# Linear attention and a routed feed-forward block on one core: y's product placed between kv and M, and the first k weights on another queue

## The chip, the core and the metric

The kernel runs on one core of a Trainium2 chip. A core has a matrix engine (TensorE, in the profile PE, its weight loads PEld), a vector engine (VectorE, DVE), a scalar engine (ScalarE, ACT), GpSimd (POOL) and SyncE (SP), which here only issues DMAs. Each engine takes its instructions in order, and they wait for each other by semaphores. Products land in PSUM, a small memory of banks, and have to be evicted from there by VectorE or ScalarE. The metric is the device time of one execution in microseconds, lower is better.

## What is computed

The input x has 2048 tokens of 640 values, in bf16. Three things are added up: x, a linear attention of the normalized x, and a routed block which again gives x, plus an update for eight tokens.

```python
xn = _layernorm(x)
# A: 32 heads of 20
q, k, v = split(xn @ wqkv)
phi = lambda t: jnp.where(t > 0, t + 1, jnp.exp(t)) + 1e-6
kv  = einsum("bhsd,bhse->bhde", phi(k), v)
z   = einsum("bhsd->bhd", phi(k))
a   = (einsum(phi(q), kv) / (einsum(phi(q), z) + 1e-6)) @ wo
# B: the 8 tokens with the largest r = xn @ w_r
sel = xn[argsort(-r)[:8]]
y   = ((silu(sel @ w_gate) * (sel @ w_up)) @ w_down) * sigmoid(r_sel)
b   = xn + scatter(y to the 8 tokens)
out = x + a + b
```

## The kernel before

The tokens are worked in 16 tiles of 128 (`T`, index t), the 640 columns in 5 chunks (`KC`).

**The start.** Loads go out on two queues: SP's (`nc.sync.dma_start`) and ScalarE's (`nc.scalar.dma_start`), L104 to L113. The k weights `wk` come in two pieces: chunks 2 to 4 on ScalarE's queue (L108), chunks 0 and 1 on SP's (L109). Each tile is normalized: VectorE takes statistics of the two halves (`ln_half`, L163) and joins them (`ln_aggr`, L167); the root and, from tile 2 on, the reciprocal are made on GpSimd (L171 to L179), for tiles 0 and 1 (`LN_FAST`) partly on VectorE (L171 for tile 0, L175, L189); `ln_norm` (L191) writes xn. TensorE needs the transposed xnT: tiles 0 to 2 are transposed on TensorE (`tr_tile`, L200) and evicted (`tr_evict`, L206), later tiles by a transposing DMA on SP (L196). One column of wk holds w_r, put there through a small product (L287, L288).

**The loop** over t has k = xn wk (L236), the Gram products ga of phi(k) and xn (L259), and q (L248); ScalarE makes exp and relu (L213, L216) and VectorE joins them (L225). SP also issues the later loads in a fixed order, between the transposes (`late_loads`, L343), and writes xn + x to a copy in DRAM, xcp (L363). The Gram matrix GT = xn^T phi(k) takes the place of v: kv is then wv^T GT.

**The last third** runs in the order in which it is written. Selection of the eight tokens on VectorE and GpSimd; gbA and gbC (L489, L590), the rest of the Gram matrix; gate and up of the eight tokens (gu, L606); hm, transposed on TensorE as ph after tile 8 of gbC (L642) and multiplied into hT (L643). GT's last columns are evicted from gbC on ScalarE (L650). Then y = hT wd (py, 48 products, L655), copied on VectorE (L663), and added by an indirect DMA from GpSimd to eight rows of xcp (L664). SP then reloads x from xcp in six pieces (L669). TensorE goes on with kv in eight blocks of 80 columns (L678), evicted in three groups by VectorE into a masked, spread form kvT (L688), and M = kv wo in five chunks (L728), evicted on ScalarE and, for chunks 2 and 4, on VectorE (L743). `norm(j)` (L632) divides a quarter of phi(q) by its denominator, in place, on VectorE; four of them come before the output sums. An output block t (L749) is 5 x 2 products of pqT and M in PSUM, rotating over four places (A, B, the banks D0 and D1, C); VectorE adds x (L757) and a store goes out on SP or ScalarE's queue in turn (L768). The last block is worked in three pieces (L770 to L776).

Of the kernel before, what the change touches and what calls it, by code (L numbers as in the profile page):

```python
# [8 lines left out]
P = 128  # L9
S = 2048  # L10
D = 640
# [3 lines left out]
T = S // P  # L15
KC = D // P
FC = F // P
# [27 lines left out]
def kernel(  # L45
# [62 lines left out]
    nc.scalar.dma_start(wk[:, 2:KC, 0:D], wqkv_v[:, 2:KC, D : 2 * D])  # L108
    nc.sync.dma_start(wk[:, 0:2, 0:D], wqkv_v[:, 0:2, D : 2 * D])  # L109
# [55 lines left out]
    def ln_aggr(t):  # L165
# [5 lines left out]
        (nc.vector if t == 0 else nc.gpsimd).tensor_scalar(  # L171
            out=sq[:, 0:1], in0=mv[:, 1:2], scalar1=EPS_BF16, scalar2=None, op0=ALU.add
        )
        if t < LN_FAST:
            nc.vector.tensor_copy(sc[:, 0:1], mv[:, 0:1])  # L175
# [28 lines left out]
    def tr_evict(t, ptr, lo, hi, copy):  # L204
        src = ptr[:, 0:D].rearrange("p (k f) -> p k f", k=KC)
        copy(xnT[:, lo:hi, t * P : (t + 1) * P], src[:, lo:hi, :])  # L206
# [81 lines left out]
    nc.scalar.copy(wk[:, :, D], prep[:, 0:KC])  # L288
    ln_half(1, 1)
    ln_aggr(1)  # L290
    ln_half(2, 0)
    ln_half(2, 1)
    ln_norm(1)
# [86 lines left out]
    tr_evict(1, tr1a, 0, 2, nc.vector.tensor_copy)  # L380
    tr_tile(1, tr1b, 2, KC)
    tr_evict(1, tr1b, 2, KC, nc.scalar.copy)
# [255 lines left out]
    for t in range(2, 9):  # L638
        gb2(t)
# [8 lines left out]
    for t in range(9, T):  # L648
        gb2(t)
    nc.scalar.copy(GT[:, :, TBLK:D], gbC[:, 0:D].rearrange("p (c f) -> p c f", c=KC))  # L650
    py = bank("D0", "py")
    for fc in range(FC):
        j, b = fc // 3, fc % 3
        for i in range(4):
            nc.tensor.matmul(  # L655
                py[32 * i : 32 * i + 32, 0:QW],
                lhsT=hT[:, 4 * b + j, :],
                rhs=wd[:, fc, i * QW : (i + 1) * QW],
                start=(fc == 0), stop=(fc == FC - 1),
                tile_position=(0, 32 * i),  # L660
            )
    y_sb = sb([P, QW], BF16, "y_sb")
    nc.vector.tensor_copy(y_sb[:], py[:, 0:QW])  # L663
    nc.gpsimd.indirect_dma_start(  # L664
        out=xcp[:], out_offset=bass.IndirectOffsetOnAxis(ap=rowu[:, 0:1], axis=0),
        in_=y_sb[:], in_offset=None, compute_op=ALU.add,
    )
    for a, b in ((0, 1), (1, 2), (2, 4), (4, 8), (8, 12), (12, 16)):
        nc.sync.dma_start(x_sb[:, a:b, :], xcp_v[:, a:b, :])  # L669


    pkv = (bank("D1", "pkv0"), bank("D0", "pkv1"), pair("B", "pkv2"))
    groups = (range(0, NEB, 2), (1, 3), (5, 7))
# [12 lines left out]
    def kv_evict(i):  # L686
        n, lo, w = len(groups[i]), groups[i][0], KC * 2 * PAD
        nc.vector.tensor_tensor(  # L688
            out=kvT[:, PAD : PAD + NEB * w].rearrange("e (b m c) -> e b m c", b=NEB, m=KC)[
                :, lo : groups[i][-1] + 1 : 2, :, 0:PAD  # L690
# [9 lines left out]
    norm(0)  # L700

# [18 lines left out]
    pm = {}  # L720

    def m_pass(m, i):
        if i == 0:
            pm[m] = Acc("CABDC"[m], f"M{m}")
        for a, b in halves:
            for g in range(4):
                o = PAD + ((2 * g + i) * KC + m) * 2 * PAD - i * PAD
                nc.tensor.matmul(  # L728
                    pm[m].at(a, b)[32 * g : 32 * g + 32, :],
                    lhsT=kvT[:, o : o + 2 * PAD],  # L730
                    rhs=wo[:, 2 * g + i, a:b],
                    start=(i == 0), stop=(i == 1),
                    tile_position=(0, 32 * g),
                )

    m_pass(0, 0)
    m_pass(1, 0)
    for m in range(KC):
        if m > 1:
            m_pass(m, 0)  # L740
        m_pass(m, 1)
        for a, b in pm[m].spans:
            (nc.vector.tensor_copy if m in (2, 4) else nc.scalar.copy)(M[:, m, a:b], pm[m].at(a, b))  # L743
    for j in range(1, NTB):
        norm(j)
# [13 lines left out]
    for t in range(T):  # L759
        o_t = work.tile([P, D], BF16, tag=("ek", "rk", "eq", "rq")[t % 4], name=f"o_t{t}")  # L760
        if t < T - 1:
            po = Acc("ABDC"[t % 4], f"o{t}")
# [5 lines left out]
            (nc.sync, nc.scalar)[t % 2].dma_start(out_v[:, t, :], o_t[:])  # L768
        else:
# [41 lines left out]
```

## Time and profile before

| | us |
|---|---|
| median of three runs | 113.37 (113.35 to 115.64) |
| the profiled execution | 113.7 |
| its span in the profile | 112.0 |
| TensorE busy | 105.6 (94%) |
| VectorE busy | 85.8 (77%) |
| ScalarE busy | 54.9 (49%) |
| GpSimd busy | 40.2 (36%) |

The span runs from the first to the last recorded instruction or transfer; 1.7 us of the execution lie outside it. A row of the timeline gives the start in us from the span's beginning, the length in us, the engine, the line, the operation, its output and input tiles, the shapes and how many are merged in the row; in brackets stands how long the engine sat idle before it, and what ended that. A row of a transfer with "KB" gives its size and the time from issue to landing. PSUM and SBUF tiles are named as in the code. An engine with "q" behind its name (SPq, ACTq) is its instruction queue, where DMAs are issued.

### The profile page before, as it was taken

The numbers are of one execution on the slowest core, as the hardware profiler recorded it, in microseconds if no ns is written. First come the engines' busy times: TensorE is split into PE (matmuls) and PEld (weight loads), VectorE is DVE, ScalarE is ACT, GpSimd is POOL, SyncE is SP. The second block draws the span as 40 slices with busy tenths as digits, with TensorE's granted clock in tenths as the row PEclk, the third lists the DMA queues.
The fourth block names the chain that finished last, engine by engine and source line by source line (L and its number), as shares of the span: only waits on it lengthen the run. The fifth ranks groups of instructions, "written<-read, shape, count | busy, mean of one in ns | idle before, by whom it ended". The sixth has DMA issues, their size and how long they took to land.

```text
span 112.0 us, 3000 instructions
## 1 busy us (share of the span) xinstructions
PE 105.6 (94%) x1183; PEld 69.5 (62%) x1183; DVE 85.8 (77%) x199; ACT 54.9 (49%) x101; POOL 40.2 (36%) x90
## 2 busy tenths in 40 slices
PE   6889999999799999999999999999999999999990
PEld 2345866777377766777766644358886555555560
DVE  6898799887998889867999887933139999756581
ACT  4038987777577787777977745086016000000000
POOL 5328495998799757590000000430051000000000
PEclk9999999999999999999999999999999999999999
DMA  3998179997989999996999730039322799943333
GB/s 77 328 376 272 30 112 343 216 273 154 148 191 322 252 115 298 277 305 181 292 372 385 279 117 4 0 117 310 112 81 21 214 341 378 336 147 117 117 117 117
DMA packets 25359, 23.09 MB, mean 206 GB/s; under 512 B 10625, under 2 KB 24065, under 8 KB 25345
## 3 DMA queue, kind: packets, MB, share of 16 engines
q1 hardware_dynamic: 22784, 20.53, 67.9%
q10 hardware_dynamic: 2384, 2.33, 6.0%
q0 software_dynamic: 176, 0.04, 0.6%
q8 instruction: 9, 0.15, 0.6%
q14 instruction: 6, 0.04, 0.1%
HBM read 14.94 MB, written 5.81 MB: 185 GB/s over the span
## 4 chain that ended last, share of the span: by engine, by line
PE 65%; DMA 10%; issue 9%; DVE 7%; ACT 2%; SPq 2%; POOL 1%; POOLq 0%; DVEq 0%
PE q L248 20%; PE k L236 19%; PE o L749 10%; PE gaC L259 6%; DMA wk<-in_A_wqkv_dram 4%; PE gaD L259 3%; DMA xcp<-y_sb,rowu 3%; DMA x_sb<-xcp 3%; PE gbA L489 2%; DVE o_t L757 2%; DVE pqT L632 1%; SPq L669 1%; PE zp L462 1%; PE o14a L749 1%; PE o10a L749 1%
## 5 line engine op out<-in xcount | busy, mean ns | idle before, releaser
L248 PEld LDWEIGHTS <-wq 128*128 128x128 bf16 x400 | 24.3, 117 | 3.5 <-issue 0.2
L236 PE MATMUL k<-wk,xnT 128*128 128x512 bf16 (+1 forms) x160 | 24.7, 300 | 1.5 <-ACT eq L213 0.8
L248 PE MATMUL q<-xnT,wq 128*128 128x128 bf16 x400 | 24.9, 219 | 0.0
L749 PEld LDWEIGHTS <-pqT 128*128 128x128 bf16 x165 | 12.8, 98 | 9.7 <-issue 0.4
L236 PEld LDWEIGHTS <-xnT 128*128 128x128 bf16 x160 | 12.5, 98 | 9.7 <-DMA xnT<-xn 0.9
L225 DVE SCALAR_TENSOR_TENSOR pk<-ek,rk 128x640 bf16<-128x640 bf16 x16 | 13.2, 824 | 4.4 <-ACT rk L216 4.2
L213 ACT ACTIVATE eq<-q 128x640 bf16<-128x640 f32 x16 | 11.2, 703 | 10.3 <-PE q L248 10.3
L749 PE MATMUL o<-M,pqT 128*128 128x512 bf16 x110 | 15.8, 299 | 0.3 <-DVE o_t L757 0.3
L163 DVE BATCH_NORM_STATS2 st<-x_sb 128x6 f32<-128x320 bf16 x32 | 14.1, 479 | 0.3 <-DMA x_sb<-in_A_x_dram 0.3
L225 DVE SCALAR_TENSOR_TENSOR pqT<-eq,rq 128x640 bf16<-128x640 bf16 x16 | 13.2, 823 | 0.2 <-ACT rq L216 0.2
L176 POOL TENSOR_TENSOR sq<-sq,half 128x1 bf16<-128x1 bf16 x16 | 12.4, 776 | 2.3 <-DVE sc L175 1.0
L213 ACT ACTIVATE ek<-k 128x640 bf16<-128x640 f32 x16 | 11.3, 705 | 2.2 <-PE k L236 1.1
L757 DVE TENSOR_TENSOR o_t<-o,x_sb 128x640 bf16<-128x640 f32 x11 | 8.8, 820 | 3.2 <-PE o L749 3.2
L178 POOL TENSOR_TENSOR sc<-sq,neg 128x1 f32<-128x1 bf16 x14 | 10.9, 776 | 1.1
L216 ACT ACTIVATE rq<-q 128x640 bf16<-128x640 f32 x16 | 11.2, 700 | 0.0
L216 ACT ACTIVATE rk<-k 128x640 bf16<-128x640 f32 x16 | 11.2, 699 | 0.0
L537 POOL COPY xsT<-xnT 128x5 bf16 x8 | 2.3, 353 | 21.2 <-DVE icol L551 21.2
L259 PE MATMUL gaC<-pk,xn 128*128 128x512 bf16 x32 | 9.5, 378 | 0.0
L191 DVE TENSOR_SCALAR xn<-x_sb,sc 128x640 bf16<-128x640 bf16 (+2 forms) x17 | 6.9, 409 | 2.2 <-POOL sc L179 2.1
L171 POOL TENSOR_SCALAR sq<-mv 128x1 bf16<-128x1 bf16 x15 | 4.7, 311 | 9.0 <-DVE mv L167 9.0
L489 PE MATMUL gbA<-pk,xn 128*128 128x512 bf16 x32 | 7.3, 380 | 0.0
L360 DVE TENSOR_TENSOR x_sb<-x_sb,xn 128x640 bf16<-128x640 bf16 x16 | 7.0, 482 | 0.0
(152 smaller groups left out, 118.6 us busy)
## 6 DMA issues: line engine op xcount, KB each, us to landing
xcp<-x_sb SPq DMA_DIRECT2D x4, 640.0 KB, 4.1
x_sb<-in_A_x_dram SPq DMA_DIRECT2D x3, 640.0 KB, 6.0
wd<-in_B_w_down_dram SPq DMA_DIRECT2D x2, 960.0 KB, 6.6
x_sb<-xcp SPq DMA_DIRECT2D x3, 640.0 KB, 6.8
wg<-in_B_w_gate_dram SPq DMA_DIRECT2D x2, 768.0 KB, 6.0
wu<-in_B_w_up_dram SPq DMA_DIRECT2D x2, 768.0 KB, 5.5
out_dram<-o_t SPq DMA_DIRECT2D x8, 160.0 KB, 2.3
out_dram<-o_t ACTq DMA_DIRECT2D x7, 160.0 KB, 1.9
```

Source lines behind the costliest of these rows:

```text
L163: nc.vector.bn_stats(out=stat[t][:, h, :], in_=x_sb[:, t, h * HW : (h + 1) * HW])
L176: nc.gpsimd.tensor_tensor(out=sq[:, 1:2], in0=sq[:, 0:1], in1=half[:], op=ALU.pow)
L178: nc.gpsimd.tensor_tensor(out=sc[:, 1:2], in0=sq[:, 1:2], in1=neg1[:], op=ALU.pow)
L213: nc.scalar.activation(e[:], ps[:, 0:D], AF.Exp)
L216: nc.scalar.activation(r[:], ps[:, 0:D], AF.Relu)
L225: nc.vector.scalar_tensor_tensor(out=dst, in0=ea, scalar=1.0, in1=ra, op0=ALU.min, op1=ALU.add)
L236: nc.tensor.matmul(ps[:, a:b], lhsT=xnT[:, kc, t * P : (t + 1) * P], rhs=wk[:, kc, a:b], start=(kc == 0), stop=(kc == KC - 1),)
L248: nc.tensor.matmul(ps[:, m * P : (m + 1) * P], lhsT=wq[:, kc, m::KC], rhs=xnT[:, kc, t * P : (t + 1) * P], start=(kc == 0 and m in (0, 4)) ...
L259: nc.tensor.matmul(gaC[:, c * TBLK : (c + 1) * TBLK] if c < 2 else gaD[:], lhsT=xn[:, t, c * P : (c + 1) * P], rhs=pk[:, t, 0:TBLK], start ...
L489: nc.tensor.matmul(gbA[:, (c - 3) * TBLK : (c - 2) * TBLK], lhsT=xn[:, t, c * P : (c + 1) * P], rhs=pk[:, t, 0:TBLK], start=(t == 0), stop ...
L749: nc.tensor.matmul(ps, lhsT=pqT[:, m, t * P : (t + 1) * P], rhs=M[:, m, a:b], start=(m == 0), stop=(m == KC - 1),)
L757: nc.vector.tensor_tensor(out=o_t[:, a:b], in0=ps, in1=x_sb[:, t, a:b], op=ALU.add)
```

## The change

Several edits are made together.

- At the start, chunks 0 to 2 of wk are loaded on ScalarE's queue and chunks 3 and 4 on SP's. The sum under tile 1's root is made on VectorE, as tile 0's; the casts of the means of tiles 0 and 1 are made on ScalarE. The copy of the w_r column comes behind the statistics of tile 1 in the text, which puts it behind tile 1's cast on ScalarE. Tile 1 is normalized between the two halves of tile 2's statistics. The two evictions of tile 1's transposition change engines.
- hm is transposed after tile 11 of gbC, not after tile 8.
- y's product, its copy, the scatter and the reloads of x move from ahead of kv to behind it; the copy is made on ScalarE, and y's place in PSUM is the pair A.
- kv's blocks are grouped 0, 2, 4, then 1, 3, 5, then 6, 7, where it was 0, 2, 4, 6, then 1, 3, then 5, 7.
- M is worked one chunk at a time, without the early first pass over chunks 0 and 1.
- Norms 1 and 2 stay ahead of the output sums; norm 3 comes behind the addition of output block 4.
- The places in PSUM rotate as B, A, D, C, and of the last block's three stores the second goes out on ScalarE's queue and the third on SP's.

```diff
@@ -105,8 +105,8 @@
     nc.scalar.dma_start(x_sb[:, 0, HW:D], x_v[:, 0, HW:D])
     for t in (1, 2):
         nc.sync.dma_start(x_sb[:, t, :], x_v[:, t, :])
-    nc.scalar.dma_start(wk[:, 2:KC, 0:D], wqkv_v[:, 2:KC, D : 2 * D])
-    nc.sync.dma_start(wk[:, 0:2, 0:D], wqkv_v[:, 0:2, D : 2 * D])
+    nc.scalar.dma_start(wk[:, 0:3, 0:D], wqkv_v[:, 0:3, D : 2 * D])
+    nc.sync.dma_start(wk[:, 3:KC, 0:D], wqkv_v[:, 3:KC, D : 2 * D])
     nc.scalar.dma_start(wq[:, 2:KC, :], wqkv_v[:, 2:KC, 0:D])
     nc.sync.dma_start(x_sb[:, 3, :], x_v[:, 3, :])
     nc.sync.dma_start(wq[:, 0:2, :], wqkv_v[:, 0:2, 0:D])
@@ -168,11 +168,11 @@
         sc = work.tile([P, 2], F32, tag="sc", name=f"sc{t}", bufs=4)
         sq = work.tile([P, 2], BF16, tag="sq", name=f"sq{t}", bufs=4)
         scal[t] = sc, sq
-        (nc.vector if t == 0 else nc.gpsimd).tensor_scalar(
+        (nc.vector if t < LN_FAST else nc.gpsimd).tensor_scalar(
             out=sq[:, 0:1], in0=mv[:, 1:2], scalar1=EPS_BF16, scalar2=None, op0=ALU.add
         )
         if t < LN_FAST:
-            nc.vector.tensor_copy(sc[:, 0:1], mv[:, 0:1])
+            nc.scalar.copy(sc[:, 0:1], mv[:, 0:1])
         nc.gpsimd.tensor_tensor(out=sq[:, 1:2], in0=sq[:, 0:1], in1=half[:], op=ALU.pow)
         if t >= LN_FAST:
             nc.gpsimd.tensor_tensor(out=sc[:, 1:2], in0=sq[:, 1:2], in1=neg1[:], op=ALU.pow)
@@ -285,12 +285,12 @@
     tr_evict(0, trb, 2, KC, nc.scalar.copy)
     prep = bank("D0", "prep").bitcast(BF16)
     nc.tensor.transpose(prep[:, 0:KC], wrow[:], ident[0:KC, 0:KC])
-    nc.scalar.copy(wk[:, :, D], prep[:, 0:KC])
     ln_half(1, 1)
     ln_aggr(1)
+    nc.scalar.copy(wk[:, :, D], prep[:, 0:KC])
     ln_half(2, 0)
+    ln_norm(1)
     ln_half(2, 1)
-    ln_norm(1)
     ln_aggr(2)
 
     iof = sb([P, 32], F32, "iof")
@@ -377,9 +377,9 @@
     kp = k_mm(0, "A")
     tr1a, tr1b = bank("D1", "tr1a").bitcast(BF16), pair("C", "tr1b").bitcast(BF16)
     tr_tile(1, tr1a, 0, 2)
-    tr_evict(1, tr1a, 0, 2, nc.vector.tensor_copy)
+    tr_evict(1, tr1a, 0, 2, nc.scalar.copy)
     tr_tile(1, tr1b, 2, KC)
-    tr_evict(1, tr1b, 2, KC, nc.scalar.copy)
+    tr_evict(1, tr1b, 2, KC, nc.vector.tensor_copy)
     ln_stats(3)
     ker = k_phi(0, kp)
     kp = k_mm(1, "B")
@@ -635,7 +635,7 @@
             op=ALU.mult,
         )
 
-    for t in range(2, 9):
+    for t in range(2, 12):
         gb2(t)
     ph = bank("D1", "ph").bitcast(BF16)
     for b in range(3):
@@ -645,32 +645,13 @@
         in0=ph[:, 0:FJ].rearrange("p (n c) -> p n c", c=32)[:, :, 0:C],
         in1=gtb[:].unsqueeze(1).to_broadcast([P, FC, C]), op=ALU.mult,
     )
-    for t in range(9, T):
+    for t in range(12, T):
         gb2(t)
     nc.scalar.copy(GT[:, :, TBLK:D], gbC[:, 0:D].rearrange("p (c f) -> p c f", c=KC))
-    py = bank("D0", "py")
...
-    for a, b in ((0, 1), (1, 2), (2, 4), (4, 8), (8, 12), (12, 16)):
-        nc.sync.dma_start(x_sb[:, a:b, :], xcp_v[:, a:b, :])
-
-
-    pkv = (bank("D1", "pkv0"), bank("D0", "pkv1"), pair("B", "pkv2"))
-    groups = (range(0, NEB, 2), (1, 3), (5, 7))
+
+
+    pkv = (bank("D0", "pkv0"), bank("D1", "pkv1"), pair("B", "pkv2"))
+    groups = ((0, 2, 4), (1, 3, 5), (6, 7))
 
     def kv_mm(i):
         for n, b in enumerate(groups[i]):
@@ -684,10 +665,11 @@
                 )
 
     def kv_evict(i):
-        n, lo, w = len(groups[i]), groups[i][0], KC * 2 * PAD
+        n, w = len(groups[i]), KC * 2 * PAD
+        lo, step = groups[i][0], groups[i][1] - groups[i][0]
         nc.vector.tensor_tensor(
             out=kvT[:, PAD : PAD + NEB * w].rearrange("e (b m c) -> e b m c", b=NEB, m=KC)[
-                :, lo : groups[i][-1] + 1 : 2, :, 0:PAD
+                :, lo : groups[i][-1] + 1 : step, :, 0:PAD
             ],
             in0=pkv[i][0:EB, 0 : n * EB].rearrange("e (b c m) -> e b m c", b=n, m=KC),
             in1=mask80[:].rearrange("e m h j -> e m (h j)").unsqueeze(1).to_broadcast([EB, n, KC, PAD]),
@@ -698,6 +680,26 @@
         kv_mm(i)
         kv_evict(i)
     norm(0)
+
+    py = pair("A", "py")
+    for fc in range(FC):
+        j, b = fc // 3, fc % 3
+        for i in range(4):
+            nc.tensor.matmul(
+                py[32 * i : 32 * i + 32, 0:QW],
+                lhsT=hT[:, 4 * b + j, :],
+                rhs=wd[:, fc, i * QW : (i + 1) * QW],
+                start=(fc == 0), stop=(fc == FC - 1),
+                tile_position=(0, 32 * i),
+            )
+    y_sb = sb([P, QW], BF16, "y_sb")
+    nc.scalar.copy(y_sb[:], py[:, 0:QW])
+    nc.gpsimd.indirect_dma_start(
+        out=xcp[:], out_offset=bass.IndirectOffsetOnAxis(ap=rowu[:, 0:1], axis=0),
+        in_=y_sb[:], in_offset=None, compute_op=ALU.add,
+    )
+    for a, b in ((0, 1), (1, 2), (2, 4), (4, 8), (8, 12), (12, 16)):
+        nc.sync.dma_start(x_sb[:, a:b, :], xcp_v[:, a:b, :])
 
     M = sb([P, KC, D], BF16, "M", tag="wq")
     halves = ((0, TBLK), (TBLK, D))
@@ -717,32 +719,24 @@
             i = a // TBLK
             return self.banks[i][:, a - i * TBLK : b - i * TBLK]
 
-    pm = {}
-
-    def m_pass(m, i):
-        if i == 0:
-            pm[m] = Acc("CABDC"[m], f"M{m}")
+    for m in range(KC):
+        pm = Acc("CBADC"[m], f"M{m}")
         for a, b in halves:
-            for g in range(4):
-                o = PAD + ((2 * g + i) * KC + m) * 2 * PAD - i * PAD
-                nc.tensor.matmul(
-                    pm[m].at(a, b)[32 * g : 32 * g + 32, :],
-                    lhsT=kvT[:, o : o + 2 * PAD],
-                    rhs=wo[:, 2 * g + i, a:b],
-                    start=(i == 0), stop=(i == 1),
-                    tile_position=(0, 32 * g),
-                )
-
-    m_pass(0, 0)
-    m_pass(1, 0)
-    for m in range(KC):
-        if m > 1:
-            m_pass(m, 0)
-        m_pass(m, 1)
-        for a, b in pm[m].spans:
-            (nc.vector.tensor_copy if m in (2, 4) else nc.scalar.copy)(M[:, m, a:b], pm[m].at(a, b))
-    for j in range(1, NTB):
-        norm(j)
+            for i in range(2):
+                for g in range(4):
+                    o = PAD + ((2 * g + i) * KC + m) * 2 * PAD - i * PAD
+                    nc.tensor.matmul(
+                        pm.at(a, b)[32 * g : 32 * g + 32, :],
+                        lhsT=kvT[:, o : o + 2 * PAD],
+                        rhs=wo[:, 2 * g + i, a:b],
+                        start=(i == 0), stop=(i == 1),
+                        tile_position=(0, 32 * g),
+                    )
+        copy = nc.vector.tensor_copy if m in (2, 4) else nc.scalar.copy
+        for a, b in pm.spans:
+            copy(M[:, m, a:b], pm.at(a, b))
+    norm(1)
+    norm(2)
 
 
     def out_mm(t, ps, m, a, b):
@@ -759,21 +753,23 @@
     for t in range(T):
         o_t = work.tile([P, D], BF16, tag=("ek", "rk", "eq", "rq")[t % 4], name=f"o_t{t}")
         if t < T - 1:
-            po = Acc("ABDC"[t % 4], f"o{t}")
+            po = Acc("BADC"[t % 4], f"o{t}")
             for m in range(KC):
                 for a, b in halves:
                     out_mm(t, po.at(a, b), m, a, b)
             for a, b in po.spans:
                 out_add(t, po.at(a, b), o_t, a, b)
             (nc.sync, nc.scalar)[t % 2].dma_start(out_v[:, t, :], o_t[:])
+            if t == 4:
+                norm(3)
         else:
             for i in range(3):
                 a, b = LAST[i : i + 2]
-                ps = pair("CAB"[i], f"o_last{i}")[:, 0 : b - a]
+                ps = pair("CBA"[i], f"o_last{i}")[:, 0 : b - a]
                 for m in range(KC):
                     out_mm(t, ps, m, a, b)
                 out_add(t, ps, o_t, a, b)
-                (nc.scalar, nc.sync, nc.scalar)[i].dma_start(out_v[:, t, a:b], o_t[:, a:b])
+                (nc.scalar, nc.scalar, nc.sync)[i].dma_start(out_v[:, t, a:b], o_t[:, a:b])
 
 
 def two(ap):
```

42 lines of the change are left out of this document (19 added, 23 removed).

## The prediction

> **What bounds the kernel now.** I read the page's busy times first, then TensorE's waits, then its weight loads in order of time.
>
> ```profile
> span 112.0 us, 3000 instructions
> ```
>
> ```profile
> PE 105.6 (94%) x1183; PEld 69.5 (62%) x1183; DVE 85.8 (77%) x199; ACT 54.9 (49%) x101; POOL 40.2 (36%) x90
> ```
>
> TensorE is at work in 94% of the span. The change takes no product away, so it can gain only what TensorE waits, and lose only what it makes TensorE wait. The longest wait of the products in the main loop (who waited for whom, total, times, longest), and the weight load of the same product (start, length, engine, line, operation, count, idle before it):
>
> ```profile
> PE k L236 <- ACT eq L213: 0.8, 1, 0.8
> ```
>
> ```profile
> 28.91 1.16 PEld L236 LDWEIGHTS <-xnT 128*128 128x128 bf16 x9 [0.94 <-DMA xnT<-xn]
> ```
>
> The product's row names a ScalarE operation; the load's row names what really came last. TensorE stood still in front of k of tile 6, for an xnT that a transposing DMA brings. The list has no other stop in the loop behind it. The other waits stand at the start, and in the last third:
>
> ```profile
> 78.62 0.17 PEld L642 LDWEIGHTS <-hm 128*128 128x128 bf16 x3 [0.24 <-DVE hm L617]
> ```
>
> ```profile
> 80.85 0.81 PEld L655 LDWEIGHTS <-hT 128*32 128x32 bf16 x48
> 81.79 1.61 PEld L678 LDWEIGHTS <-wv 128*80 128x80 bf16 x40
> 83.45 0.39 PEld L728 LDWEIGHTS <-kvT 80*32 80x32 bf16 x16
> 84.20 2.25 PEld L728 LDWEIGHTS <-kvT 80*32 80x32 bf16 x64 [0.36 <-DVE kvT L688]
> 86.71 5.49 PEld L749 LDWEIGHTS <-pqT 128*128 128x128 bf16 x41 [0.27 <-DVE M L743]
> 92.64 0.37 PEld L749 LDWEIGHTS <-pqT 128*128 128x128 bf16 x3 [0.44 <-issue]
> ```
>
> Four gaps: 0.24 ahead of hm's transposition, 0.36 inside M, 0.27 ahead of the output sums, and 0.44 ahead of output block 4, whose bank is block 0's and so is held until block 0's sum is added to x.
>
> **The start.** wk's two loads: issue and us to landing of ScalarE's, then SP's with its time from issue to landing, and the product that waits for it.
>
> ```profile
> 1.26 0.45 ACTq L108 DMA_DIRECT2D wk<-in_A_wqkv_dram  x1
> ```
>
> ```profile
> wk<-in_A_wqkv_dram ACTq DMA_DIRECT2D x1, 480.0 KB, 4.2
> ```
>
> ```profile
> 2.18 4.64 DMA wk<-in_A_wqkv_dram
> ```
>
> ```profile
> 6.87 1.53 PE L236 MATMUL k<-wk,xnT 128*128 128x512 bf16 x10 [0.50 <-DMA wk<-in_A_wqkv_dram]
> ```
>
> ScalarE's load lands at 5.5, SP's at 6.8, and TensorE had waited 0.50 for SP's. With chunks 0 to 2 on ScalarE's queue, k of tile 0 starts at 6.4; chunks 3 and 4, due three products later at about 7.0 (ten take 1.53), have landed by then. It starts 0.47 earlier. The two casts now on ScalarE find it without other work, and the first product that needs the w_r column comes a whole half of k later: nothing.
>
> What is late next is xn of tile 1. VectorE's rows, and GpSimd's that give the norms of tiles 2 and 3 (eight operations without a pause: the first two and the last):
>
> ```profile
> 6.54 0.15 DVE L175 CAST sc<-mv 128x1 f32<-128x1 bf16 x1
> 6.62 0.88 DVE L163 BATCH_NORM_STATS2 st<-x_sb 128x6 f32<-128x320 bf16 x2
> 7.55 0.16 DVE L189 RECIPROCAL sc<-sq 128x1 f32<-128x1 bf16 x1
> 7.75 0.45 DVE L191 TENSOR_SCALAR xn<-x_sb,sc 128x640 bf16<-128x640 bf16 x1
> 8.11 0.20 DVE L167 BATCH_NORM_AGGREGATE mv<-st 128x2 bf16<-128x12 f32 x1
> ```
>
> ```profile
> 8.40 0.22 POOL L171 TENSOR_SCALAR sq<-mv 128x1 bf16<-128x1 bf16 x1 [0.88 <-DVE mv L167]
> 8.71 0.57 POOL L176 TENSOR_TENSOR sq<-sq,half 128x1 bf16<-128x1 bf16 x1
> ```
>
> ```profile
> 11.65 0.18 POOL L179 CAST sc<-mv 128x1 f32<-128x1 bf16 x1
> ```
>
> The sum for tile 1's root moves from GpSimd to VectorE and takes the cast's place at 6.54 (0.15). The root (0.57) can then begin near 6.8 and end near 7.4; reciprocal and normalizing follow as now, 0.20 apart: 7.6 to 8.05, where 8.20 stands now. So TensorE, 0.47 early with k of tile 0, keeps at most 0.15 of it at k of tile 1. I take 0.15 as its lead from there.
>
> The price is behind it. The second half of tile 2's statistics (half of 0.88) now stands behind the normalizing of tile 1, so the aggregate comes at 8.05 + 0.44 = 8.49 in place of 8.11, nearly 0.4 later. GpSimd's eight operations have no pause between 8.40 and 11.83: all of them shift, and with them the normalizing of tile 3 and the first transposing DMA on SP.
>
> ```profile
> 12.34 2.12 SPq L196 DMA_TRANSPOSE xnT<-xn  x1
> ```
>
> ```profile
> 22.79 1.21 SPq L196 DMA_TRANSPOSE xnT<-xn  x1
> ```
>
> ```profile
> xnT<-xn SPq DMA_TRANSPOSE x1, 6.1
> ```
>
> ```profile
> xnT<-xn SPq DMA_TRANSPOSE x13, 3.8
> ```
>
> SP issues in order; everything up to the transpose of tile 6 goes out behind 12.34. That transpose, issued at 22.79, needs 6.1 us and lands at 28.9, where k of tile 6 waits; the median of all thirteen is 3.8. I read the difference as a backlog on the queue. If it is one, its end moves with its beginning, and k of tile 6 starts 0.38 later. If the transpose hangs on its own issue alone, VectorE has four tiles to catch up in, and at best TensorE's lead of 0.15 is kept. Between +0.38 and −0.15 I take **+0.38**, because 6.1 against 3.8 is nearest to the backlog.
> The Trainium skill (DMA: Bandwidth & Descriptors, Queues, rings and completion order) says that on each DMA engine the descriptors of a ring are consumed in ring order; the 6.1 us agree with it.
>
> **The last third.** ScalarE's eviction of gbC, VectorE's rows, GpSimd's scatter:
>
> ```profile
> 80.96 0.69 ACT L650 CAST GT<-gbC 128x640 bf16<-128x640 f32 x1 [3.57 <-PE gbC L590]
> ```
>
> ```profile
> 82.79 0.49 DVE L688 TENSOR_TENSOR kvT<-pkv,mask 80x320 bf16<-80x320 f32 x1 [0.55 <-PE pkv L678]
> 83.83 0.55 DVE L688 TENSOR_TENSOR kvT<-pkv,mask 80x160 bf16<-80x160 f32 x2 [0.55 <-PE pkv L678]
> 84.30 1.48 DVE L632 TENSOR_TENSOR pqT<-pqT,rb 128x2560 bf16<-128x2560 bf16 x1
> ...
> 87.57 4.28 DVE L632 TENSOR_TENSOR pqT<-pqT,rb 128x2560 bf16<-128x2560 bf16 x3
> 91.77 0.82 DVE L757 TENSOR_TENSOR o_t<-o,x_sb 128x640 bf16<-128x640 f32 x1
> ```
>
> ```profile
> 82.55 1.75 POOL L664 DMA_INDIRECT xcp<-y_sb,rowu  x1 [8.71 <-DVE y_sb L663]
> ```
>
> - hm's transposition moves behind 15 more gbC products: the 0.24 goes, and kv starts at 80.61, where y would have.
> - Six blocks of kv read only columns of GT below 512; blocks 6 and 7, now last, wait for gbC's eviction. Its 0.69 lie beside the 30 products ahead (three quarters of 1.66). Without that cover it costs 0.69 and the 0.11 until it starts.
> - y's 48 products (0.94, from 80.85 to 81.79) now stand between kv and M, and cover kvT's last eviction: kv to 82.27, y to 83.21. The 0.36 goes; M, 3.26 from 83.45 to 86.71, takes 2.90 and ends at 86.11.
> - the 0.27: M's third copy, which that row names, no longer follows a norm that ends at 85.78. But the first output product doesn't read that copy; the gap may be TensorE's own run-out. Between 0 and 0.27 I take 0.1: output block 0 starts at 86.0.
> - the norms: with two, not three, ahead of the first addition, VectorE is ready for it near 86.9 + 2.9 = 89.8, not 91.85.
>
> Gained: 0.24 + 0.36 + 0.1 + 0.44 = **1.14**, the last if block 0's addition ends before TensorE comes to block 4, 5.5 behind block 0, at 91.5. Here y is the danger. Its products end 1.42 later (83.21 for 81.79), and so does its copy, which is ScalarE's now and ahead of M's copies there; with it move the scatter (82.55 to 83.97) and the six reloads of x, all on SP ahead of the output stores:
>
> ```profile
> 85.93 0.33 SPq L669
> ```
>
> ```profile
> x_sb<-xcp SPq DMA_DIRECT2D x1, 160.0 KB, 2.2
> ```
>
> ```profile
> 87.71 1.57 SPq L669 DMA_DIRECT2D x_sb<-xcp  x3
> ```
>
> ```profile
> x_sb<-xcp SPq DMA_DIRECT2D x1, 640.0 KB, 5.5
> ```
>
> Block 0 landed at 85.93 + 2.2 = 88.1, now 89.5; its addition runs from 89.8 to 90.6, 0.9 ahead of need. Blocks 4 to 7 landed at 87.71 + 5.5 = 93.2, now 94.6. Then come block 4's addition (0.82), norm 3 (1.48, new at this place) and block 5's addition, to 97.7; block 9 needs that bank at 91.5 + 5 × 1.37 (a quarter of 5.49) = 98.3. **The slack is 0.6**, and each us beyond it is paid in full. The last store leaves on SP instead of ScalarE, behind the same addition: nothing.
>
> One row speaks against this order. While the scatter held GpSimd, VectorE stood idle from 83.28 to 83.83, and norm 0 started just as the scatter ended (84.30). Now norm 0 runs from about 82.7 to 84.2, and the scatter is due at 83.97 in it.
> The Trainium skill (SBUF — State Buffer, Who interferes with whom) says that a VectorE instruction with two SBUF inputs contends with a GpSimd instruction that reads SBUF, and that the one which starts first holds the port for its whole length; by it the scatter would wait until 84.2, which is inside the slack.
>
> **Sum.** −1.14 + 0.38 = −0.76. The profiled execution took 113.7 (112.0, and 1.7 around it), 0.33 more than the median of 113.37: 112.9 on its scale, **112.6** on the median's. About 2% (2.3 us) is what a measurement of this kernel can tell from no change.
>
> **Rivals.**
> 1. There is no backlog and TensorE keeps its lead: −1.14 − 0.15 = −1.29, so 112.1. For it: the queue's later issues may catch up; against it: 6.1 us. Chance 0.2.
> 2. The output stores, earlier now, share the DMA engines with the reload of blocks 4 to 7. Two stores of 160 KB through ScalarE's queue are half of its 640 KB; half of the 3.3 us that it took beyond a single block's 2.2 are 1.6 us, 1.0 beyond the slack: 113.6. Against it: the reload may be ahead of them. Chance 0.2.
> 3. **Slower than before**: the scatter, asked for amid VectorE's norms and copies, doesn't get through beside them. This decides from 0.6 + 0.76, some 1.4 us of delay. Held until M's last copy ends (86.11 + 0.8 = 86.9), it is 2.9 late, block 9 waits 2.3, and the time is 114.9. For it: the idle 0.55 beside the scatter; against it: norm 0 is over 0.2 after the scatter asks. Chance 0.1.
> 4. kv waits for the whole of GT after all: 0.8 lost, nothing gained, 113.4. Against it: the program's waits name the eviction of gbC only for block 6. Chance 0.05.
>
> **Chances.** The forecast has 0.45 (112.3 to 112.9). The range, 111.8 to 113.7, takes in the forecast and rivals 1, 2 and 4, and leaves out 3 and the corners. Faster by over 2% would need gains that no row shows: 0.05. Slower by over 2% needs a scatter held for some 3.5 us: 0.06. Within 2%: 0.89.
>
> **What would show it.** In the profile after: k of tile 0 near 6.4, GpSimd's eight operations ending near 12.2, k of tile 6 near 29.3 (rival 1: 28.8); no wait ahead of hm's transposition or inside M, kv directly behind gbC, no wait at output block 4. From k of tile 6 to output block 0 57.1 us for 57.8, to block 4 62.6 for 63.73. The forecast is wrong if block 9 waits for block 5's addition, if the scatter begins over 1 us behind y's copy, or if k of tile 6 starts by 28.9.

## The result, and the profile after

The changed kernel has a median of 111.94 us (17 executions, 111.72 to 113.14), the kernel before, beside it, 113.47 us (17 executions). The ratio is 0.988, with an interval of 0.984 to 0.991: 1.4 us less, within 2%. The ratios here and below leave out executions over 1.5% slower than the kernel's fastest, and what is gained or lost in us is worked out from the ratios, so it can differ a little from the difference of the medians, which are of all executions. A second session gave less: 112.63 us (12 executions, 111.94 to 113.19) beside 113.19, a ratio of 0.994 (0.991 to 0.998), 0.65 us. Both signs agree, and the sizes lie around the forecast's 0.993. Why they differ is a large part of what follows.

The page after, its head and its busy times:

```profile
span 110.3 us, 3004 instructions
...
PE 105.2 (95%) x1183; PEld 69.1 (63%) x1183; DVE 85.3 (77%) x197; ACT 55.3 (50%) x104; POOL 38.9 (35%) x89
```

TensorE works as long as before, to 0.4 us (105.6); the span is 1.7 shorter. As the prediction said, only waits could go. TensorE's waits after (who waited for whom, total, times, longest):

```profile
PE warm L271 <- DVE zero L117: 1.0, 1, 1.0
PE k L236 <- DMA xnT<-xn: 0.3, 1, 0.3
PE k L236 <- ACT xnT L206: 0.3, 1, 0.3
...
```

Nothing of the last third is left in the list. TensorE's weight loads after, in order of time (start, length, line, count, idle before it):

```profile
28.38 1.22 PEld L236 LDWEIGHTS <-xnT 128*128 128x128 bf16 x10 [0.45 <-DMA xnT<-xn]
...
78.65 0.21 PEld L642 LDWEIGHTS <-hm 128*128 128x128 bf16 x3
79.94 1.63 PEld L659 LDWEIGHTS <-wv 128*80 128x80 bf16 x40
81.61 0.81 PEld L688 LDWEIGHTS <-hT 128*32 128x32 bf16 x48
82.39 2.02 PEld L728 LDWEIGHTS <-kvT 80*32 80x32 bf16 x58
84.57 0.66 PEld L728 LDWEIGHTS <-kvT 80*32 80x32 bf16 x22 [0.16 <-issue]
85.34 21.76 PEld L743 LDWEIGHTS <-pqT 128*128 128x128 bf16 x165
```

kv (L659) follows gbC with no wait ahead of hm's transposition, y (L688) follows kv, M follows y, and the 165 loads of the output sums run without a stop: the waits of 0.24, 0.36 and 0.44 are gone, and of the 0.27 ahead of output block 0 there are 0.11 left (84.57 + 0.66 to 85.34). k of tile 6 stands at 28.38, where it stood at 28.91. The last addition of the kernel, on VectorE, in the timeline after:

```profile
106.69 0.94 DVE L751 TENSOR_TENSOR o_t<-o_last,x_sb 128x320 bf16<-128x320 f32 x3
```

To see what of this is the change's, both kernels were executed anew. The same rows of the kernel before:

```profile
28.30 1.22 PEld L236 LDWEIGHTS <-xnT 128*128 128x128 bf16 x10 [0.34 <-DMA xnT<-xn]
...
80.28 0.81 PEld L655 LDWEIGHTS <-hT 128*32 128x32 bf16 x48
81.22 1.61 PEld L678 LDWEIGHTS <-wv 128*80 128x80 bf16 x40
82.88 2.56 PEld L728 LDWEIGHTS <-kvT 80*32 80x32 bf16 x80
85.70 5.49 PEld L749 LDWEIGHTS <-pqT 128*128 128x128 bf16 x41 [0.27 <-DVE M L743]
91.65 2.27 PEld L749 LDWEIGHTS <-pqT 128*128 128x128 bf16 x17 [0.45 <-issue]
```

And of the changed kernel:

```profile
29.00 1.22 PEld L236 LDWEIGHTS <-xnT 128*128 128x128 bf16 x10 [1.16 <-DMA xnT<-xn]
...
80.55 1.63 PEld L659 LDWEIGHTS <-wv 128*80 128x80 bf16 x40
82.23 0.81 PEld L688 LDWEIGHTS <-hT 128*32 128x32 bf16 x48
83.00 2.78 PEld L728 LDWEIGHTS <-kvT 80*32 80x32 bf16 x80
85.89 21.75 PEld L743 LDWEIGHTS <-pqT 128*128 128x128 bf16 x165
```

Differences of starts in these rows (the last additions start at 108.53 and 107.53 before, 106.69 and 107.23 after):

| us | before, first | before, anew | after, first | after, anew |
|---|---|---|---|---|
| k of tile 6 starts at | 28.91 | 28.30 | 28.38 | 29.00 |
| to the first product behind gbC | 51.94 | 51.98 | 51.56 | 51.55 |
| y and kv, to M | 2.60 | 2.60 | 2.45 | 2.45 |
| M, to output block 0 | 3.26 | 2.82 | 2.95 | 2.89 |
| output sums, to the last addition | 21.82 | 21.83 | 21.35 | 21.34 |
| k of tile 6 to the last addition | 79.62 | 79.23 | 78.31 | 78.23 |

Two readings. From k of tile 6 on, the change gains 0.9 to 1.4 us, and does so in each pairing. M's wait of 0.36, which stood in the first profile of before, does not stand in the second of the same program: there M's 80 loads take 2.56 without a gap. The two experiments below that keep the old last third (the start alone, and the moved load) don't have it either; there the loads take 2.56 and 2.57. And k of tile 6 itself moves by 0.6 between two executions of one program, in either kernel. No single pair of profiles can tell 0.5 us there.

### The profile page after: what moved, and what is told of

Its sections match the earlier page's. It is cut to its first block, busy times and chain, and to the rows that moved or that the text cites. A ratio compares the mean times of both kernels' runs of the same rounds, so it can differ in the third digit from the quotient of the medians.

```text
span 110.3 us, 3004 instructions
## 1 busy us (share of the span) xinstructions
PE 105.2 (95%) x1183; PEld 69.1 (63%) x1183; DVE 85.3 (77%) x197; ACT 55.3 (50%) x104; POOL 38.9 (35%) x89
## 4 chain that ended last, share of the span: by engine, by line
PE 70%; DVE 12%; DMA 7%; POOL 6%; issue 2%; DVEq 0%; POOLq 0%
PE o L743 14%; PE k L236 13%; PE q L248 13%; PE gbA L489 6%; DMA xnT<-xn 5%; PE gaC L259 4%; PE gbC L590 4%; DVE st L163 4%; POOL sq L176 3%; DVE xn L191 2%; PE gaD L259 2%; DMA x_sb<-in_A_x_dram 2%; PE M L728 2%; PE gu L606 2%; POOL sc L178 2%
## 5 line engine op out<-in xcount | busy, mean ns | idle before, releaser
L178 POOL TENSOR_TENSOR sc<-sq,neg 128x1 f32<-128x1 bf16 x14 | 9.2, 657 | 1.1
```

Source lines behind the costliest of these rows:

```text
L178: nc.gpsimd.tensor_tensor(out=sc[:, 1:2], in0=sq[:, 1:2], in1=neg1[:], op=ALU.pow)
```

## The experiments

The disputed points were: what the edits of the start cost, since k of tile 6 came earlier where the prediction had it later; whether the gains of the last third are those that the prediction named; and where the slack ends. All ratios are to the kernel before, run beside it. Its median is 113.14 us for the start alone, all but the start, before again and the moved load; 113.52 for hm early, y ahead of kv, norm 3 behind block 7 and the last combination; and 113.19 for the others.

### The start alone

The kernel before with the change's edits of the start and nothing else.

```diff
-    nc.scalar.dma_start(wk[:, 2:KC, 0:D], wqkv_v[:, 2:KC, D : 2 * D])
-    nc.sync.dma_start(wk[:, 0:2, 0:D], wqkv_v[:, 0:2, D : 2 * D])
+    nc.scalar.dma_start(wk[:, 0:3, 0:D], wqkv_v[:, 0:3, D : 2 * D])
+    nc.sync.dma_start(wk[:, 3:KC, 0:D], wqkv_v[:, 3:KC, D : 2 * D])
...
-    ln_half(2, 1)
-    ln_norm(1)
+    ln_norm(1)
+    ln_half(2, 1)
```

> The kernel before with the edits of the start alone (wk's chunks, the sum and casts of tiles 0 and 1, the order of tile 2's statistics, tile 1's evictions); the last third is as it was. Theory A (the prediction's): the first transposing DMA goes out later, a backlog carries this to tile 6, and the kernel is some 0.4 us slower. Theory B (the start's edits are what moved k of tile 6 from 28.91 to 28.38): 0.5 us faster. Theory C (k of tile 6 waits for a transfer whose landing varies by some tenths from one execution to the next, whatever the start does): within 0.2 us of before, and k of tile 6 anywhere from 28.3 to 29.

Measured: 113.28 us, ratio 1.0022 (1.0004 to 1.0040), a quarter of a us slower. In its profile k of tile 0 stands at 6.52, k of tile 1 at 9.03, the first transposing DMA at 12.90, and k of tile 6 at 28.18. The time says a small loss, and the one profile doesn't show it; but it is the profile of the fastest of the twelve executions (112.60 us).

### All but the start

The changed kernel with the start as before.

```diff
-    nc.scalar.dma_start(wk[:, 0:3, 0:D], wqkv_v[:, 0:3, D : 2 * D])
-    nc.sync.dma_start(wk[:, 3:KC, 0:D], wqkv_v[:, 3:KC, D : 2 * D])
+    nc.scalar.dma_start(wk[:, 2:KC, 0:D], wqkv_v[:, 2:KC, D : 2 * D])
+    nc.sync.dma_start(wk[:, 0:2, 0:D], wqkv_v[:, 0:2, D : 2 * D])
...
-    ln_norm(1)
-    ln_half(2, 1)
+    ln_half(2, 1)
+    ln_norm(1)
```

> The kernel before with all edits but those of the start. Theory A: 1.1 us faster. Theory B: the whole gain less 0.5, some 1.0 faster. Theory C: nearly the whole gain, 1.3 to 1.5 faster. In all of them the stretch from k of tile 6 to output block 0 is 57.0 us, where it was 57.8, and output block 4 waits for nothing.

Measured: 112.12 us, ratio 0.9922 (0.9901 to 0.9942), 0.9 faster. Output block 0 stands 56.91 behind k of tile 6, as in the whole change (56.96 and 56.89). The gain is the last third's, and the two parts add up: −0.9 + 0.25 = −0.65, which is what the whole change gave in the second session. They do not reach the 1.4 of the first. The six executions lie between 112.00 and 112.30.

### The kernel before, again

No edit; the rows are shown above.

> The kernel before, unchanged, for a second profile of it. Theories A and B: k of tile 6 starts at 28.9 again, within 0.1. Theory C: it starts somewhere else by some tenths, and the landing time of tile 6's transposing DMA, 6.1 us, differs by as much. The time is that of before, within the interval.

Measured: 112.92 us, ratio 1.0012 (0.998 to 1.0044). Tile 6's transposing DMA, issued at 22.79 as in the first profile, took 5.5 us to land, not 6.1. So 0.6 us at k of tile 6 are one program's spread.

### The load ahead of tile 6's transpose moved behind it

SP issues the load of x for tiles 12 to 15 (640 KB) right ahead of that transposing DMA. Here it goes out behind it, and each later load one tile later.

```diff
-            3: (x_sb, x_v, 12, 16), 4: (wo, wo_v, 0, 4), 5: (wo, wo_v, 4, 8),
+            4: (x_sb, x_v, 12, 16), 5: (wo, wo_v, 0, 4), 6: (wo, wo_v, 4, 8),
```

> The kernel before with the load of x's tiles 12 to 15 issued behind tile 6's transposing DMA and not ahead of it, and each later load one tile later. If tile 6's transpose is late because 640 KB stand ahead of it on the queue, it lands in 3.5 to 4 us, k of tile 6 follows q of tile 5 without a wait (28.1), and the kernel is 0.8 us faster, or less if tile 7's transpose now waits in its place. If the backlog reaches back to the first transpose, or the transpose is slow for itself, it still needs 5 us or more and the time stays.

Measured: 112.82 us, ratio 0.9972 (0.9945 to 0.9999), 0.3 faster. The DMAs and the loads of TensorE in this kernel (the first row: time from issue to landing, in us):

```profile
xnT<-xn SPq DMA_TRANSPOSE x1, 4.3
```

```profile
27.99 1.26 PEld L236 LDWEIGHTS <-xnT 128*128 128x128 bf16 x10
...
29.82 0.31 PEld L259 LDWEIGHTS <-xn 128*128 128x128 bf16 x2 [0.36 <-issue]
```

The transpose lands in 4.3 in place of 5.5 to 6.1, and k of tile 6 no longer waits. But the Gram product behind it, at 29.82, now stands 0.36; in the list of waits it stands as gaC, 0.2, for phi(k) from VectorE. The gain over a good landing is given back there: k of tile 7 starts at 31.81, and at 31.72 in the second profile of before. What remains is that ten of the twelve executions lie between 112.76 and 112.89: without the late landing the spread is nearly gone here. It is small in all but the start too, though, where the load stands ahead.

### The whole change, again

No edit; the rows are shown above.

> The changed kernel unchanged, beside the kernel before in the same session. If the parts add up as measured alone (the start's edits +0.2 us, all others -0.9 us), it is 0.6 to 0.7 us faster than before, a ratio near 0.994. If the first comparison's ratio of 0.988 is the kernels' own, 1.4 us faster. Its profile: output block 0 56.9 to 57.0 us behind k of tile 6 again, no wait ahead of hm's transposition, inside M or at output block 4; if the landing of tile 6's transposing DMA varies from one execution to the next, k of tile 6 stands anywhere from 28.0 to 29.0.

Measured: ratio 0.9942 (0.9906 to 0.9978). Between the first profile and this, the span grows from 110.3 to 110.9, and k of tile 6 moves from 28.38 to 29.00: it is all there. The issues on SP in this profile, and the landing of the transpose issued at 22.68:

```profile
12.90 1.98 SPq L196 DMA_TRANSPOSE xnT<-xn  x1
...
21.11 0.58 SPq L343 DMA_DIRECT2D x_sb<-in_A_x_dram  x1
22.68 1.21 SPq L196 DMA_TRANSPOSE xnT<-xn  x1
```

```profile
xnT<-xn SPq DMA_TRANSPOSE x1, 6.3
```

In the first profile after, it was issued at 22.77 and took 5.6. In the first session ten of 17 executions lie between 111.72 and 112.03, and seven between 112.36 and 113.14. In the second, five of twelve lie under 112.2 and seven between 112.6 and 113.2. The two sessions differ in how many executions fall into the upper group.

### Norm 3 ahead of the output sums

```diff
+    norm(3)
...
-            if t == 4:
-                norm(3)
```

> The changed kernel with norm 3 ahead of the output sums, as before the change. If the wait at output block 4 came from the third norm ahead of block 0's addition, as the prediction had it, block 0's addition moves from 89.06 to 90.5 and ends at 91.3, and block 4, due at 90.8, waits 0.5: 0.4 to 0.5 us slower than the changed kernel. If the wait at block 4 came from the whole order of the last third (y's place, the groups of kv), no difference.

Measured: 112.9 us, ratio 0.9983 (0.9944 to 1.0021), 0.27 more in the median than the changed kernel beside it, which the intervals can't tell apart. The profile can. Its loads of the output sums:

```profile
85.20 5.49 PEld L744 LDWEIGHTS <-pqT 128*128 128x128 bf16 x41
91.15 2.81 PEld L744 LDWEIGHTS <-pqT 128*128 128x128 bf16 x21 [0.45 <-issue]
```

The wait at output block 4 is back with its 0.45. It was the third norm ahead of block 0's addition, as predicted.

### hm transposed early

```diff
-    for t in range(2, 12):
+    for t in range(2, 9):
...
-    for t in range(12, T):
+    for t in range(9, T):
```

> The changed kernel with hm transposed after tile 8 of gbC, as before the change. The prediction's term of 0.24 us: TensorE waits 0.2 to 0.3 us ahead of hm's transposition again, and the time is 0.24 us more than the changed kernel's. If the wait is given back behind it (gbC's eviction on ScalarE, kv's last blocks), no difference.

Measured: 113.25 us, ratio 0.9951 (0.9919 to 0.9984). Two rows of its loads:

```profile
29.35 1.22 PEld L236 LDWEIGHTS <-xnT 128*128 128x128 bf16 x10 [1.36 <-DMA xnT<-xn]
...
79.06 0.17 PEld L642 LDWEIGHTS <-hm 128*128 128x128 bf16 x3 [0.24 <-DVE hm L617]
```

The 0.24 is back and isn't given back: from k of tile 6 to the last addition (107.92) are 78.57, against 78.31 and 78.23. That k of tile 6 stands at 29.35 here has nothing to do with hm, which comes 50 us later. Three of its executions take 112.1, nine 113.2 to 113.5, and so its median says little about 0.24.

### y ahead of kv again

The block of y's product, copy, scatter and reloads is moved back ahead of kv; everything else stays as changed.

```diff
+    py = pair("A", "py")
...
     pkv = (bank("D0", "pkv0"), bank("D1", "pkv1"), pair("B", "pkv2"))
...
-    py = pair("A", "py")
```

> The changed kernel with y's product, copy, scatter and reload back ahead of kv. If y covers kvT's last eviction, as the prediction had it, M now waits 0.4 to 0.6 us for kvT and this is 0.4 to 0.6 us slower than the changed kernel, though the scatter and the reload come 1.6 us earlier. If kv's order alone did away with the wait in M, there is no wait, and the time is the changed kernel's or, if late reloads cost it time, less.

Measured: 113.35 us, ratio 1.0005 (0.9978 to 1.0032): the whole gain is gone. TensorE's loads, then VectorE's evictions of kvT:

```profile
79.84 0.81 PEld L657 LDWEIGHTS <-hT 128*32 128x32 bf16 x48
80.79 1.61 PEld L679 LDWEIGHTS <-wv 128*80 128x80 bf16 x40
82.44 0.10 PEld L728 LDWEIGHTS <-kvT 80*32 80x32 bf16 x3
83.51 2.72 PEld L728 LDWEIGHTS <-kvT 80*32 80x32 bf16 x77 [0.97 <-DVE kvT L690]
```

```profile
81.59 0.41 DVE L690 TENSOR_TENSOR kvT<-pkv,mask 80x240 bf16<-80x240 f32 x1 [2.55 <-PE pkv L679]
82.82 0.64 DVE L690 TENSOR_TENSOR kvT<-pkv,mask 80x240 bf16<-80x240 f32 x2 [0.82 <-PE pkv L679]
```

After three loads M stands for 0.97, until the two last evictions (82.82 to 83.46) are through. Worked a chunk at a time and with kv's last blocks apart, M needs y ahead of it much more than before's order did, twice as much as I had put down. Which of the two makes it so was not tried apart. From k of tile 6 (28.14) to the last addition (107.67) it takes 79.53, 1.3 more than the changed kernel's 78.23: 1.0 of it between M and output block 0, and 0.3 ahead of M (51.70 and 2.60, where the table has 51.55 and 2.45).

### The scatter held up

A copy of y, a copy of a column and three roots stand between y's copy and the scatter on GpSimd.

```diff
     nc.scalar.copy(y_sb[:], py[:, 0:QW])
+    nc.gpsimd.tensor_copy(y_sb2[:], y_sb[:])
+    nc.gpsimd.tensor_copy(dly[:, 0:1], y_sb2[:, 0:1])
+    for _ in range(3):
+        nc.gpsimd.tensor_tensor(out=dly[:, 1:2], in0=half[:], in1=half[:], op=ALU.pow)
     nc.gpsimd.indirect_dma_start(
...
-        in_=y_sb[:], in_offset=None, compute_op=ALU.add,
+        in_=y_sb2[:], in_offset=None, compute_op=ALU.add,
```

> The changed kernel with some 2.1 us of work on GpSimd put between y's copy and the scatter (one copy of y, one of a column and three roots of 0.57 us each). The output stays the reference's. Prediction's reckoning, a slack of 0.6 us at output block 9 and each us beyond it paid in full: 1.5 us slower than the changed kernel. By the profile of the changed kernel the first to be late is output block 4 (block 0's addition ended 0.9 us ahead of its need) and block 9 has 1.1 us: 1.0 to 1.2 us slower, with the wait at block 4 and none of its own at block 9. If the additions catch up wholly: no slower.

Measured: 115.08 us, ratio 1.0169 (1.0104 to 1.0235). GpSimd's row of the scatter, then TensorE's loads:

```profile
86.21 1.75 POOL L703 DMA_INDIRECT xcp<-y_sb,rowu  x1 [0.36 <-issue]
```

```profile
81.82 0.81 PEld L688 LDWEIGHTS <-hT 128*32 128x32 bf16 x48
...
85.48 5.49 PEld L749 LDWEIGHTS <-pqT 128*128 128x128 bf16 x41
92.89 16.30 PEld L749 LDWEIGHTS <-pqT 128*128 128x128 bf16 x124 [1.91 <-issue]
```

In the first profile of the changed kernel the scatter starts 1.67 behind y's first load (83.28 and 81.61), here 4.39: 2.72 late, more than the 2.1 that I had meant. Output block 4 waits 1.91, so its slack was 0.8, near the 0.9 that the changed kernel's profile had shown; block 9 has no wait of its own. From k of tile 6 (28.59) to the last addition (108.77) it takes 80.18, 1.95 more than the changed kernel's 78.23. In this profile the late scatter is paid in full beyond its slack, but it is paid at block 4, not at block 9. The profiled execution (114.18) is the fastest of the five, and the median is 2.4 above the changed kernel's in the same session; where the other executions lose the rest no profile shows.

### Norm 3 behind output block 7

```diff
-            if t == 4:
+            if t == 7:
                 norm(3)
```

> The changed kernel with norm 3 behind the addition of output block 7, not 4. Block 5's addition, which frees the bank of block 9, then comes straight behind block 4's: its slack grows from 1.1 us to 2.5 us. If executions of the changed kernel lose time at block 9 because the reload of blocks 4 to 7 lands late in some of them (rival 2), the median falls by 0.3 to 0.6 us and the executions lie closer together. If the spread comes from tile 6's transposing DMA in the loop, no difference from the changed kernel, and the same spread.

Measured: 112.44 us, ratio 0.9903 (0.9866 to 0.9939), six executions from 111.87 to 113.0. In its profile k of tile 6 stands at 29.37, its transpose landed in 6.6 us, and the span is 111.3. Behind k of tile 6 this leaves 81.9, as in the two profiles of the changed kernel (110.3 − 28.38 and 110.9 − 29.00). Room at block 9 alone changes nothing there; the spread stays, and in the three profiles it is set ahead of k of tile 6.

### A combination: no edits at the start, the load of x moved

The start is undone as in the second experiment, and in addition:

```diff
-            3: (x_sb, x_v, 12, 16), 4: (wo, wo_v, 0, 4), 5: (wo, wo_v, 4, 8),
+            4: (x_sb, x_v, 12, 16), 5: (wo, wo_v, 0, 4), 6: (wo, wo_v, 4, 8),
```

> The change without its edits at the start, and with one more: the load of x for tiles 12 to 15 goes out behind tile 6's transposing DMA on SP and not ahead of it, each later load one tile later. If the gains are independent, they add: -0.9 us (the change without the start, measured alone) and -0.3 us (the load moved, measured alone): 1.2 us faster than before, a ratio near 0.989. If tile 6's wait is only given back later in the loop, no better than 0.9 us faster.

Measured: 112.17 us, ratio 0.9899 (0.9851 to 0.9947), 1.1 faster of the 1.2 that would add up, so within the interval the gains add. Its timeline, TensorE's loads and VectorE:

```profile
98.22 9.50 PEld L743 LDWEIGHTS <-pqT 128*128 128x128 bf16 x74 [0.59 <-issue]
```

```profile
95.21 0.82 DVE L751 TENSOR_TENSOR o_t<-o,x_sb 128x640 bf16<-128x640 f32 x1 [1.78 <-DMA x_sb<-xcp]
95.95 1.48 DVE L632 TENSOR_TENSOR pqT<-pqT,rb 128x2560 bf16<-128x2560 bf16 x1
97.35 0.82 DVE L751 TENSOR_TENSOR o_t<-o,x_sb 128x640 bf16<-128x640 f32 x1
```

Here block 4's addition waits 1.78 for the reload, norm 3 follows, block 5's addition ends at 98.17, and block 9 starts at 98.22, 0.59 late. This is the place that rival 2 named. The reloads of 640 KB have a median landing of 8.6 us here, where the changed kernel's was 6.5. This execution, at 112.69, is the slowest of the seven.

### The combination with norm 3 behind block 7

To the edits of the combination comes:

```diff
-            if t == 4:
+            if t == 7:
                 norm(3)
```

> The change without its edits at the start, the load of x for tiles 12 to 15 behind tile 6's transpose, and norm 3 behind block 7's addition. The same kernel with norm 3 behind block 4's addition lost 0.59 us at block 9 in its profile, to a reload that landed 8.6 us after its issue. If that wait is what kept it at 112.2, 0.5 us faster than that: a ratio to before near 0.985, and no wait of a product in the output sums. If not, near 0.990 again.

Measured: 112.04 us, ratio 0.9886 (0.9849 to 0.9922). No product waits in its output sums, and k of tile 6 stands at 28.22 without a wait. Four of its six executions lie between 112.02 and 112.06. The 0.5 us expected over the combination before did not come: the ratios differ by 0.0013, and their intervals overlap. A late reload like the one above thus isn't what sets the median. This kernel is no faster than the changed one at its best (111.72), and by the intervals not to be told from it; most of its executions lie close together. So do those of all but the start, and so this doesn't show that the moved load is what does it.

## Why the prediction was right, and where it wasn't

**Right: what can be gained.** The gain is TensorE's idle time ahead of the last addition, and not a shorter product. The last third, forecast at −1.14, gave −1.31 between the first two profiles and −1.00 between the second two.

- hm's 0.24: confirmed. Undoing it alone brings a wait of 0.24 back, and 0.3 us at the end.
- Output block 4's 0.44: confirmed. Norm 3 ahead of the sums brings 0.45 back, in the profile and at the end (78.72, from 28.31 to 107.03, against 78.23).
- "From k of tile 6 to output block 0 57.1, to block 4 62.6": 56.96 and 56.89; block 4 comes 41 loads of 5.49 behind block 0, so 62.4.
- kv directly behind gbC: yes (79.94), so rival 4, that kv waits for all of GT, fell.
- VectorE and the scatter: the scatter began 0.3 behind y's copy, inside norm 0, so rival 3 fell. GpSimd, ScalarE and VectorE after:

```profile
83.28 1.79 POOL L697 DMA_INDIRECT xcp<-y_sb,rowu  x1 [9.95 <-ACT y_sb L696]
```

```profile
82.68 0.29 ACT L696 CAST y_sb<-py 128x160 bf16<-128x160 f32 x1 [1.80 <-PE py L688]
```

```profile
81.97 1.48 DVE L632 TENSOR_TENSOR pqT<-pqT,rb 128x2560 bf16<-128x2560 bf16 x1
...
93.52 0.82 DVE L751 TENSOR_TENSOR o_t<-o,x_sb 128x640 bf16<-128x640 f32 x1 [0.33 <-DMA x_sb<-xcp]
94.26 1.48 DVE L632 TENSOR_TENSOR pqT<-pqT,rb 128x2560 bf16<-128x2560 bf16 x1
95.66 0.82 DVE L751 TENSOR_TENSOR o_t<-o,x_sb 128x640 bf16<-128x640 f32 x1
```

y's copy ends at 82.97, and the scatter starts at 83.28, while norm 0 runs until 83.45. So the scatter didn't stand until the norm's end, as the prediction had it by the port rule of the Trainium skill (SBUF — State Buffer, Who interferes with whom). The norm is no longer than before (1.48), and the scatter takes 1.79 where it took 1.75. The Trainium skill isn't contradicted: further down in the same section it says, as an inference, that a tensor_tensor takes only the read interface of the shared port and that descriptor generation needs the write interface. The prediction applied the rule where these rows show no wait.

**Right in mechanism, off in size: y's cover and M.** The 0.36 was a row of one execution; the same program executed again hadn't it. On the other hand y covers more than that in the new order: taken away, M stands 0.97. Against the usual profile of before, M to output block 0 gains nothing (2.82 to 2.89): of the 0.27 ahead of the output sums, 0.16 went (I took 0.1), but M's 80 loads, worked a chunk at a time, take 2.78 in place of 2.56. That left about 1.0, not 1.31, for the last third where before doesn't have M's wait.

Part of this 1.0 stood in no term of the sum. Between the second profiles it is made up of 0.43 up to the first product behind gbC (hm's 0.24, and 0.19 more), 0.15 in y and kv, and 0.49 in the output sums, less 0.07 in M. With y ahead of kv again, 0.15 came back in the first stretch and 0.15 in the second. So about 0.3 of the gain belongs to kv's place ahead of y: the loads follow each other with smaller gaps in that order (y to kv 0.13 before, kv to y 0.05 after). Why, no run shows. That the last third came out near the forecast is thus in part luck: 0.46 was put down for M and the gap behind it, of which nothing is left against the second profile of before, and 0.34 came that wasn't put down.

**Right in kind, wrong in place: the slack.** The prediction put the danger at block 9, with 0.6. The slack there was 1.1 in the first profile after: block 5's addition ends at 96.48 (95.66 + 0.82), and block 9 is due at 85.34 + 9 × 1.36 = 97.6. The first to be late is block 4, with 0.8, for which the prediction had 0.9. Rival 2's wait, the reload landing late, stood once in a profile, with 0.59 where it was priced at 1.0, in another kernel than the changed one.

**Wrong: the backlog.** This step let a delay at the first transposing DMA travel along the queue, to k of tile 6 at +0.38. Up to the first transpose it held, and more than it: the aggregate of tile 2 came at 8.73 (8.49 forecast), GpSimd's eight operations ended at 12.47 (12.2), and the transpose was issued 0.65 later. SP's issues after, and the 640 KB load in the first profile of before:

```profile
12.99 1.57 SPq L196 DMA_TRANSPOSE xnT<-xn  x1
...
22.77 1.21 SPq L196 DMA_TRANSPOSE xnT<-xn  x1
```

```profile
20.65 0.58 SPq L343 DMA_DIRECT2D x_sb<-in_A_x_dram  x1
```

Tile 6's transpose is issued at 22.77, and was at 22.79: the 0.65 is used up by then. In all fourteen profiles this issue stands 12.25 to 12.28 behind the start of q of tile 0, whichever start the kernel has: it goes with the pace of the loop, not with the first transpose. k of tile 6, at 28.38, gave the sign by which the prediction called this step wrong (by 28.9); at 29.00, in the second profile of the same kernel, it would not have given it. What keeps it beyond its issue is the 640 KB load right ahead of it; with that load behind it, it lands in 4.1 to 4.3 us in place of 5.5 and more. The rule quoted from the Trainium skill (DMA: Bandwidth & Descriptors, Queues, rings and completion order), that a ring is consumed in order, agrees with these numbers; what stands right ahead in it counts, not what began late ten us earlier. In so far rival 1 had the mechanism (the transpose hangs on its own issue, and VectorE catches up). Its lead of 0.15 doesn't show in the first two profiles, with q of tile 0 at 10.50 and 10.53. Over all of them it does: q of tile 0 stands at 10.34 to 10.55 in the eight with the changed start and at 10.53 to 10.92 in the six with the old one, 0.2 earlier by the medians. Whether it survives depends on the landing.

Whether the start costs time at all, as forecast, isn't settled. The start alone is 0.25 us slower, and the second session's 0.65 for the whole change is as much less than the 0.9 of all but the start. But the first session's 1.4 is 0.5 more than that 0.9. The landings seen in single profiles of programs with the start as before and the load ahead are 5.5, 5.5 and 6.1, and of the eight with the changed start 5.5, 5.5, 5.6, 5.6, 5.9, 6.3, 6.5 and 6.6. That the changed start makes late landings more frequent is argued from these, and from the executions: those of all but the start lie within 0.3 us, those of the changed kernel within 1.4 and 1.3 in its two sessions. One row does move with the start: the 640 KB load goes out 2.14 ahead of the transpose in the three profiles with the old start (20.65 and 22.79 in the first) and 1.57 or 1.58 ahead in the eight with the changed one (21.11 and 22.68 in the second profile after). Whether that makes the landing late was not tried, nor which part of the start does it.

So the forecast's −1.14 + 0.38 = −0.76 lies between the two sessions' −1.4 and −0.65 by luck as well: the +0.38 has the wrong mechanism, and in place of −1.14 the runs give some −1.0, in part from another place.

## What to carry to other kernels

Profile the unchanged kernel twice before a wait of some tenths is booked as a gain: the wait at k of tile 6 and M's wait weren't properties of the program but of the execution. A product that covers an eviction is worth what stands when it is taken away, not the gap that happens to show in the old order. Where additions, norms and reloads share one engine, work out the slack of each block that reuses a bank, from the first on: the earliest is the one that a delay meets first.

## What the runs showed of the hardware that I had not expected

- One tile's transposing DMA, issued between 22.62 and 23.18 in eleven profiles with a 640 KB load right ahead of it on the queue, took from 5.5 to 6.6 us to land; in three with that load behind it, 4.1 to 4.3. k of tile 6 waits for it and so stands anywhere from 28.14 to 29.37 in the eleven. I had read 6.1 us as a property of the program.
- The first output stores of 160 KB, issued up to 97 us, landed in a median of 3.3 to 4.3 us in the two profiles before and of 6.1 to 7.4 in the two after, where the first leaves 0.3 us behind the last issue of a reload and not 3.3. That this is the reason was not tried. VectorE then waited for the stores to give back their buffers, for 1.42 in the second profile after, without cost to TensorE:

```profile
99.43 1.56 DVE L751 TENSOR_TENSOR o_t<-o,x_sb 128x640 bf16<-128x640 f32 x2 [1.42 <-DMA out_dram<-o_t]
```
